# A hand-ordered attention and feed-forward kernel: the order of pairs 0 to 17 written anew, the first block of output weights requested right behind the input weights, and fewer products of zeros

## The chip, the cores and the metric

The kernel runs on one core of one Trainium2 chip. The metric is device time in microseconds. The kernel before takes 400.86 us, the median of three runs (400.78 to 400.98).

## The reference

Cosine attention for 8 batches and 12 heads, 448 positions, head size 64; then a feed-forward layer with a hard-swish over the 3584 rows of the attention's result.

```python
q_n = q / (norm(q, axis=-1) + 1e-6); k_n = k / (norm(k, axis=-1) + 1e-6)
attn = softmax(q_n @ k_n.T / 0.1)            # 448 x 448 for each head
x = (attn @ v) laid out as (8 * 448, 768)
h = x @ w_in                                 # 768 -> 2048
g = h * clip(h + 3, 0, 6) / 6
out = g @ w_out                              # 2048 -> 768
```

## The kernel before, in words

**Work.** Two heads of one batch make a pair; there are 48 pairs, six to a batch. The attention runs pair by pair, and the feed-forward layer of a batch runs in small units between later pairs. TensorE (PE) does all products and most transposes, ScalarE (ACT) the exponentials, VectorE (DVE) and GpSimd (POOL) most of the rest. SyncE (SP) issues the loads.

**The order is written out by hand.** Each engine executes its instructions in the order in which the program issues them, and the program issues them by tokens. Up to pair 17 the tokens stand in the text `PLAN`; from pair 18 (`FIRST`) on a loop produces them. A token is an operation and its arguments, and the letters v, p and a name the engine: DVE, POOL, ACT.

- `LQ.j` (L199) loads the queries or keys of item j in one 448 KB transfer; two items, 2d and 2d+1, serve the pairs 2d and 2d+1. `LV.d` (L214) loads the values of two pairs in four transfers. There are seven raw buffers: `LQ.j` waits until an earlier item's `NM` has read its buffer.
- `SQ.j.e.c.n` (L225 on ACT, L227 on POOL) squares n of seven columns from column c on; `RE.j` (L242, DVE) sums the squares; `BN`, `BS` (L248 to L254) do both by moments for three columns of item 1. `NO.d` (L278 to L285) takes the inverse norms of two items: a logarithm and an exponential on ACT, then two small operations on DVE (with v) or on ACT. `NM.j.e` (L295) multiplies an item by them. `VC.i` (L312, L314) casts the values of a pair.
- `TR.j` (L341, seven PE transposes into a PSUM bank), then `CQ.i`, `CK.i`, `CS.i` (L361, L363) copy the transposed queries and keys of pair i out of the bank. From item 14 on `XD.j` (L352) transposes by DMA instead.
- `SC.i.g` (L441, L444) are the four groups of score products of pair i, `EX.i.g` (L462, ACT) their exponentials, `VA.i.g` (L484) the products with the values into the bank pair `PV`, `FI.i` (L504, L505, DVE) the division by the sums. `BK.i` (L518, PE) and `CX.i` (L361, L363) turn the result into xT, the input of the feed-forward layer; `XP`, `XB` (L542, L530) do it by DMA.
- `UH.f.k` and `U` (L594) are the products of the feed-forward layer's first half, six to a block f of 128 columns; `UA` and `UV` do the ACT half (L611, "relu") and the DVE half (L617, "product") of the oldest open unit.
- `W` (L924, issued from POOL) requests one of twelve blocks of weights: eight of w_in, two for each quarter of its columns, then four of w_out.
- `D.n`, `DP.n`, `DQ.n` (L931, L937) are products of zeros, n of each; their result is read by nobody. DP and DQ write columns of PV that the sums leave free. A DQ works on 32-bit zeros and shows as two matmul rows in the trace.

**PSUM.** Of the eight banks two are PV. For the first six pairs four banks are the two score buffers SC0 and SC1 (two banks each, `SC.i.g.0` and `SC.i.g.1`), and Y and Z serve the transposes. At `OPEN` the SC banks become the banks M0 to M3, and all six (M0, M1, Y, Z, M2, M3; here numbered 0 to 5) go round as a ring: `SC` takes two (one for g = 3), and `TR`, `BK` and each unit one. A bank can be written again when its readers are done: for scores the exponentials on ACT, for a unit its relu on ACT and then its product on DVE.

Of the kernel before, what the change touches and what calls it, by code (L numbers as in the profile page):

```python
# [64 lines left out]
def kernel(
# [125 lines left out]
    def load_qk(j, *heads):  # L191
# [6 lines left out]
        g = slice(heads[0], heads[0] + 1) if heads else slice(0, 2)  # L198
        nc.sync.dma_start(out=raw_of[j][:, g, :, :].rearrange("p g c d -> p g (c d)"), in_=f[:, g, :])  # L199
        whole("LQ", j, heads or (0, 1))  # L200
        issued.update(("LQ", j, x) for x in heads or (0, 1))
# [916 lines left out]
```

## Time and profile before

| | |
|---|---|
| median of three runs | 400.86 us |
| the profiled execution's own time | 401.17 us |
| its span in the trace | 399.2 us |
| outside the span | 1.97 us |
| busy: PE, DVE, ACT, POOL | 98%, 74%, 69%, 59% |
| granted TensorE clock | full in all 40 slices of the page |
| matmul rows of products of zeros (L937, L931) | 65 and 1, of 3658 |

The page sums busy time over the whole span, but the kernel has a start in which queries and keys are prepared, a middle in which pairs and units alternate, and an end without attention. So the reading below is by stretches of time, each with the busy time of every engine. A busy time can hold overlaps: an instruction's start can lie before the end of the one ahead of it on the same engine, so the distance between starts is the better price of one more instruction. The chain of waits gives such distances for PE.

### The profile page before, as it was taken

How to read it: one execution, taken by the hardware profiler on the slowest of the kernel's cores; microseconds unless marked ns; L12 is line 12 of the kernel's file. 1: busy time of each engine (PE TensorE's matmuls, PEld its weight loads, DVE VectorE, ACT ScalarE, POOL GpSimd, SP SyncE). 2: the span in 40 equal slices, each digit the busy share in tenths (PEclk: the TensorE clock that was granted, in tenths of full speed). 3: DMA queues.
4: the chain of work that ended last, by engine and by line, in shares of the span. 5: the costliest groups of instructions: out<-in, count | busy, mean ns of one | idle time of the engine just before them, and what ended most of it. 6: DMA issues, size and time to landing. Idle time of an engine off the chain costs nothing.

```text
span 399.2 us, 9590 instructions
## 1 busy us (share of the span) xinstructions
PE 390.2 (98%) x3658; PEld 231.6 (58%) x3658; DVE 293.9 (74%) x537; ACT 276.9 (69%) x600; POOL 234.6 (59%) x234
## 2 busy tenths in 40 slices
PE   7999999999999999999999999999999999999996
PEld 5566556555565556555565556565565556555563
DVE  7998898999777787667767886686756566645663
ACT  5999889895768677777868769668648755235230
POOL 6999628662656988389368757767666400400070
PEclk9999999999999999999999999999999999999999
DMA  8999979988978868785887566795953423230133
GB/s 289 310 221 240 212 226 248 199 189 208 197 172 187 120 174 162 174 213 123 195 202 213 136 152 155 165 218 119 190 150 69 102 48 68 47 74 20 30 71 97
DMA packets 93165, 63.73 MB, mean 160 GB/s; under 512 B 56128, under 2 KB 93120, under 8 KB 93120
## 3 DMA queue, kind: packets, MB, share of 16 engines
q1 hardware_dynamic: 87408, 56.45, 60.4%
q0 software_dynamic: 5312, 6.29, 9.4%
q8 instruction: 28, 0.46, 0.5%
q10 hardware_dynamic: 400, 0.39, 0.3%
q14 instruction: 17, 0.14, 0.1%
HBM read 45.61 MB, written 11.01 MB: 142 GB/s over the span
## 4 chain that ended last, share of the span: by engine, by line
PE 92%; ACT 3%; DVE 2%; DMA 1%; issue 0%; POOL 0%; SPq 0%; DVEq 0%; ACTq 0%
PE M L594 25%; PE M L754 17%; PE PV L484 11%; PE Z L594 6%; PE Y L754 6%; PE M L444 5%; PE Y L594 5%; PE Z L754 5%; PE M L834 3%; ACT at L462 2%; DMA big<-in_k_dram 1%; PE Y L444 1%; PE Z L444 1%; PE Z L834 1%; PE PV L937 1%; PE SC L444 1%
## 5 line engine op out<-in xcount | busy, mean ns | idle before, releaser
L594 PE MATMUL M<-xT,w_in_sb 128*128 128x448 bf16 x540 | 114.6, 353 | 0.0
L462 ACT ACTIVATE at<-M 128x448 bf16<-128x448 f32 x195 | 96.6, 564 | 20.0 <-PE M L444 10.2
L594 PEld LDWEIGHTS <-w_in_sb 128*128 128x128 bf16 x768 | 72.2, 98 | 64.1 <-issue 3.8
L227 POOL TENSOR_TENSOR big<-big 128x896 f32<-128x896 f32 (+5 forms) x47 | 69.5, 1483 | 21.7 <-DMA big<-in_k_dram 12.0
L295 POOL TENSOR_TENSOR nrm<-big,r 128x896 bf16<-128x896 f32 (+1 forms) x45 | 75.7, 1683 | 6.5 <-ACT r L285 4.3
L617 DVE SCALAR_TENSOR_TENSOR gT<-u,M 128x448 bf16<-128x448 bf16 x80 | 49.0, 619 | 34.9 <-ACT u L611 34.3
L611 ACT ACTIVATE u<-M,bias 128x448 bf16<-128x448 f32 x90 | 58.0, 651 | 22.3 <-PE M L594 20.9
L484 PEld LDWEIGHTS <-at 128*128 128x128 bf16 (+1 forms) x1536 | 53.8, 97 | 20.5 <-issue 10.6
L484 PE MATMUL PV<-vx,at 128*128 128x65 bf16 (+1 forms) x1536 | 62.2, 193 | 0.0
L242 DVE TENSOR_REDUCE n<-big 128x14 f32<-128x896 f32 (+1 forms) x48 | 51.1, 1068 | 1.5 <-POOL big L227 1.5
L783 POOL TENSOR_TENSOR big<-big 128x384 f32<-128x384 f32 x12 | 13.0, 1080 | 58.9 <-ACT big L802 58.8
L401 POOL COPY km<-tT 64x128 bf16<-64x128 bf16 x34 | 12.8, 376 | 59.0 <-DMA tT<-nrm 24.9
L754 PEld LDWEIGHTS <-gT 128*128 128x128 bf16 x320 | 30.9, 98 | 21.4
L505 DVE TENSOR_TENSOR on<-PV,rc 128x512 bf16<-128x512 f32 x48 | 33.2, 692 | 1.7
L754 PEld LDWEIGHTS <-gs 128*128 128x128 bf16 x248 | 23.9, 98 | 16.0 <-issue 0.2
L462 ACT ACTIVATE at<-Y 128x448 bf16<-128x448 f32 x51 | 28.7, 564 | 6.1 <-PE Z L444 6.0
L754 PE MATMUL M<-w_out_sb,gT 128*128 128x384 bf16 x176 | 32.2, 326 | 0.0
L444 PE MATMUL M<-tT,kz 64*128 64x448 bf16 (+1 forms) x175 | 31.6, 351 | 0.3 <-ACT at L462 0.3
L462 ACT ACTIVATE at<-Z 128x448 bf16<-128x448 f32 x48 | 26.9, 561 | 4.2 <-PE M L444 2.1
L754 PE MATMUL M<-w_sum,gs 128*128 128x384 bf16 (+1 forms) x168 | 29.1, 318 | 0.0
L594 PE MATMUL Z<-xT,w_in_sb 128*128 128x448 bf16 x132 | 28.6, 352 | 0.0
L729 DVE TENSOR_TENSOR gs<-gT 128x1024 bf16<-128x1024 bf16 x30 | 26.3, 876 | 0.0
(135 smaller groups left out, 562.3 us busy)
## 6 DMA issues: line engine op xcount, KB each, us to landing
big<-in_k_dram SPq DMA_DIRECT2D x24, 448.0 KB, 4.4
big<-in_q_dram SPq DMA_DIRECT2D x24, 448.0 KB, 4.4
out_dram<-o SPq DMA_DIRECT2D x107, 96.0 KB, 2.2
big<-in_v_dram SPq DMA_DIRECT2D x48, 128.0 KB, 4.1
big<-in_v_dram SPq DMA_DIRECT2D x48, 96.0 KB, 4.1
w_in_sb<-in_moe_w_in_dram POOLq DMA_DIRECT2D x8, 384.0 KB, 8.3
w_out_sb<-in_moe_w_out_dram POOLq DMA_DIRECT2D x4, 768.0 KB, 11.0
tT<-nrm SPq DMA_TRANSPOSE x34, 3.2
```

What stands on the lines that cost most here:

```text
L227: engines[e].tensor_tensor(out=o, in0=i, in1=i, op=ALU.mult)
L242: nc.vector.tensor_reduce(out=sums_of(j, c0, n), in_=sq[:, :, c0 : c0 + n, :], axis=AX.X, op=ALU.add)
L295: engines[e].tensor_tensor(out=nrm[:, :, g, :].rearrange("p c g d -> p g c d"), in0=raw_of[j][:, g, :, :], in1=n2_and_r[2][:, d % 2, j % 2, :]
L444: nc.tensor.matmul(o, ks, qt[rows], start=True, stop=True)
L462: nc.scalar.activation(out=o, in_=x, func=AF.Exp, scale=inv_tau)
L484: nc.tensor.matmul(pv_out(j, h), at[rows, n, q_cols(i // HP, j)], vt[rows, 3 + h if name == "M" else 5 * h + int(name[1]), :], start=(name ...
L505: nc.vector.tensor_tensor(out=on[:, :, :, :].rearrange("p j h d -> p h j d"), in0=pv4[:, :, :, 0:D], in1=rc[:, :, :].to_broadcast([128, 2, ...
L594: nc.tensor.matmul(ps[:, 0:S], w_in_sb[:, cc, fc * 128 : (fc + 1) * 128], xT[b % 2][:, cc, 0:S], start=(cc == 0), stop=(cc == CC - 1), ski ...
L611: nc.scalar.activation(out=u[:, :], in_=ps[:, 0:S], func=AF.Relu, bias=half_bias, scale=1.0 / 6.0)
L617: nc.vector.scalar_tensor_tensor(out=g[:, fc, c0 : c0 + S], in0=u[:, :], scalar=1.0, in1=ps[:, 0:S], op0=ALU.min, op1=ALU.mult,)
L729: nc.vector.tensor_tensor(out=o[:, :, :], in0=x, in1=y, op=op)
L754: nc.tensor.matmul(m, lhs[:, c, :], rhs[:, c, c0 : c0 + width], start=(base is None and c == 0), stop=(c == KC - 1), skip_group_check=True,)
```

## The change

1. The tokens of pairs 0 to 17 stand in another order, and some work changes its engine. On ACT there are more squares (item 1's columns 3 and 4, the first half of items 5 and 7, all of item 13, but no longer those of items 8 and 15's first half), the casts of pairs 4, 8 and 9, and other copies. POOL gets the normalisation of items 11, 12 and of half of item 4, DVE gets the copies of pair 0.
2. `NO` is split into `NA` (the two ACT operations) and `NV` (the rest), so that other work can stand between them.
3. The ring of banks is no longer strictly in turn at the start: the text `RING` names a bank for each of the first allocations; after its end the ring goes round as before.
4. Products of zeros: D.1, 47 in DP and nine in DQ before; four in DP and fifteen in DQ (eleven of them first) now. The last one stands ahead of `SC.0.3`.
5. `LV.0` is issued ahead of `LQ.4`; `LQ.14`, `LV.5`, `LQ.16` and `LQ.15` ahead of `XP.6`.
6. On POOL's queue the first `W` of w_out stands behind the eighth of w_in with three operations between them, and the second nine operations further on; before, four operations stood between, and the second followed the first at once.

The rest of the edits makes the code able to do other things that this plan doesn't use (parts of a load, inverse norms in PSUM). From pair 18 on the program is unchanged.

```diff
 PLAN = [
-    "LQ.1 BN.1.0.3 DQ.9 SQ.1.p.3.2 SQ.1.a.5.2 BS.1.0.3 LQ.0 RE.1.3.4 SQ.0.p.0.3 LQ.3 SQ.3.p.0.4 SQ.0.a.3.4 RE.0 LQ.2",
-    "NO.0.1 NM.1.v.0 NM.1.v.1 SQ.3.a.4.3 NO.0.0 NM.0.p.1 SQ.2.a.4.3 TR.1.Z NM.0.p.0 LQ.5 SQ.2.a.0.4 D.1 DP.1 RE.3",
-    "CK.0.a SQ.5.p.0.4 SQ.5.a.4.3 RE.2 NO.1.v TR.0.Y LQ.4 CQ.0.a SQ.4.p.4.3 DP.2 SQ.4.a.0.4 DP.3 NM.3.p DP.1 RE.5",
-    "CQ.1.v RE.4 LV.0 SC.0.0.0 LQ.6 DP.3 VC.0.v NM.2.v.1 EX.0.0 SC.0.1.1 NM.2.p.0 CK.1.v LQ.7 LQ.8 DP.5 EX.0.1",
-    "SC.0.2.0 EX.0.2 DP.1 VC.1.v DP.1 DP.1 SC.0.3.1 EX.0.3 DP.2 VA.0.0 DP.2 LV.1 SQ.6.p.0.7 VA.0.1 SC.1.0.0 NO.2.v",
-    "NM.4.v.1 SC.1.1.1 TR.2.Y DP.1 NM.4.p.0 SQ.7.a.4.3 DP.1 RE.6 DP.1 DP.1 EX.1.0 EX.1.1 SC.1.2.0 TR.3.Z EX.1.2",
...
-    "NO.5.v BK.1.Y EX.4.3 SC.5.1.1 EX.5.0 SC.5.2.0 W TR.7.Z CX.1.v LQ.15 CK.6.v EX.5.1 VC.6.p VC.7.p EX.5.2 SC.5.3.1",
-    "CK.7.v VA.4.0 EX.5.3 VA.4.1 OPEN CS.7.v SC.6.0 EX.6.0 VA.4.2 VA.4.3.t CS.6.v FI.4 SC.6.1 EX.6.1 SC.6.2 SC.6.3",
-    "EX.6.2 TR.8 CQ.8.v BK.3 VA.5.0 CX.3.v W SQ.12.p.0.7 CQ.9.v VA.5.1 VA.5.2 VC.8.p EX.6.3 DP.1 BK.4.Y CX.4.v SC.7.0",
...
+    "LQ.1 SQ.1.a.5.2 LQ.0 BN.1.0.3 SQ.1.a.3.2 RE.1.3.4 BS.1.0.3 SQ.0.p.0.3 SQ.0.a.3.4 NA.0.1 NV.0.1 RE.0 LQ.3",
+    "SQ.3.p.0.4 NM.1.v.1 LQ.2 SQ.3.a.4.3 NM.1.v.0 NA.0.0 NV.0.0 LQ.5 RE.3 SQ.2.a.0.4 SQ.2.a.4.3 RE.2 NM.0.p.0",
+    "SQ.5.a.0.4 SQ.5.a.4.3 NM.0.p.1 DQ.11 TR.1 CK.0.v NA.1 DQ.2 TR.0 CQ.0.v DP.2 SC.0.0.0 NV.1.v LV.0 VC.0.p LQ.4",
+    "SQ.4.p.4.3 CQ.1.v SC.0.1.1 CK.1.a LQ.6 SQ.4.a.0.4 NM.3.p EX.0.0 DQ.2 SC.0.2.0 EX.0.1 DP.2 SC.0.3.1 RE.4 EX.0.2",
+    "RE.5 NM.2.v.1 NM.2.p.0 VA.0.0 LQ.8 SC.1.0.0 SQ.6.p.0.7 NA.2 NV.2.v EX.0.3 TR.3 LV.2 CK.2.v EX.1.0 SC.1.1.1 LQ.7",
+    "EX.1.1 TR.2 NM.4.p.1 VA.0.1 SC.1.2.0 NM.4.p.0 VA.0.2 EX.1.2 LV.1 W SQ.7.a.0.4 LQ.9 SQ.7.a.4.3 VA.0.3 VC.1.v",
...
+    "SC.4.3.1 EX.4.3 NM.7.p CX.2.v VC.4.a SC.5.0.0 TR.6 LV.4 EX.5.0 SC.5.1.1 RE.11 VA.4.0 CQ.6.v SC.5.2.0 EX.5.1",
+    "CQ.7.v BK.1 NV.4.v TR.7 EX.5.2 SC.5.3.1 VA.4.1 VA.4.2 LQ.13 EX.5.3 CX.1.v CK.6.v CK.7.v CS.6.v OPEN VA.4.3.t",
+    "SC.6.0 NM.8.p CS.7.v NM.9.p SC.6.1 VC.6.p SC.6.2 NA.5 EX.6.0 TR.8 SC.6.3 FI.4 CQ.9.v VA.5.0 EX.6.1 W W W CQ.8.v",
+    "BK.4 LQ.12 VA.5.1 CX.4.v BK.3 VA.5.2 CX.3.v VA.5.3.t SC.7.0 FI.5 VC.7.p EX.6.2 TR.9 EX.6.3 EX.7.0 SC.7.1 SC.7.2",
+    "EX.7.1 VA.6.0 CK.8.v EX.7.2 SC.7.3 EX.7.3 VA.6.1 LQ.14 SQ.12.p.0.7 W UH.0.0 CS.8.v BK.5 VA.6.2 CK.9.v CS.9.v",
+    "VA.6.3.t SC.8.0 CX.5.v UH.0.1 FI.6 UH.0.2 SC.8.1 EX.8.0 SC.8.2 NV.5.v EX.8.1 U UH.1.0 UH.2.0 UH.2.1 W NM.11.p.1",
+    "UH.1.1 UH.1.2 U UA SC.8.3 EX.8.2 UA UH.2.2 U NM.11.p.0 VA.7.0 UV UV VA.7.1 EX.8.3 VA.7.2 VA.7.3.t RE.12 SC.9.0",
+    "SQ.13.a.0.7 SC.9.1 EX.9.0 EX.9.1 SQ.14.p.0.7 FI.7 UH.3.0 UA UH.3.1 UH.3.2 U UA UV UV VC.8.a RE.13 U U VC.9.a UA",
+    "UA U W VA.8.0 NA.6 VA.8.1 NM.10.p VA.8.2 UV TR.10 LV.5 UV CQ.11.v SC.9.2 EX.9.2 VC.11.p VA.8.3.t SC.9.3 TR.11",
+    "NV.6.v U FI.8 VA.9.0 LQ.16 VA.9.1 UA VA.9.2 LQ.15 EX.9.3 VA.9.3.t CQ.10.v CK.10.a SQ.15.p.4.3 XP.6 NM.13.p UA",
+    "CK.11.v SC.10.0 U CS.10.v EX.10.0 RE.14.6.1 UV SC.10.1 UA CS.11.v UV VC.10.p FI.9 RE.14.0.6 SC.10.2 SQ.16.p.6.1",
...
 ]
+RING = "233232332323450123450350123451234502345012340123450125014012350123450..."
...
+        return ring[int(RING[n]) if n < len(RING) else (n - len(RING) + int(RING[-1]) + 1) % len(ring)]
...
     def norms(d, *items):
+        norms_root(d, *items)
+        norms_inverse(d, *items)
...
-    def busy(n):
-        bank_of("Y", 0)
-        for _ in range(n):
-            nc.tensor.matmul(Y[:, :], zeros[:, 0:128], zeros[:, :], start=True, stop=True)
```

More of the change, by code (lines that the diff above doesn't have):

```diff
@@ L21 @@
 PLAN = [
[39 rows of a table removed]
-]
[38 rows of a table added]
+]
+PLANNED = " ".join(PLAN).split()
+RING = "233232332323450123450350123451234502345012340123450125014012350123450123450135023451234015234501234501234501234501234501234501234501234501234501"
 @with_exitstack
@@ L157 @@
     Z = psum.tile([128, 512], FP32, name="Z", tag="Z")
-    ring = []
+    ring = [None, None, Y, Z, None, None]
     ring_n = [0]
     def next_bank():
+        n = ring_n[0]
         ring_n[0] += 1
-        return ring[(ring_n[0] - 1) % len(ring)]
+        return ring[int(RING[n]) if n < len(RING) else (n - len(RING) + int(RING[-1]) + 1) % len(ring)]
     raw_of, sq_of, nrm_of, at_of, on_of = {}, {}, {}, {}, {}
-    engines = {"v": nc.vector, "p": nc.gpsimd, "a": nc.scalar, "s": nc.sync}
+    engines = {"v": nc.vector, "w": nc.vector, "p": nc.gpsimd, "a": nc.scalar, "s": nc.sync}
     issued = set()
@@ L186, with load_qk @@
     MAIN = [0, 4, 1, 5, 2, 6]
-    def load_qk(j, *heads):
+    def load_qk(j, *part):
         needs(("NM", raw_before(j)))
@@ L197, in load_qk @@
         f = f.rearrange("n p g x -> (n p) g x")
[L198 to L201, printed above, removed]
+        c0, w = part or (0, 7)
+        o = raw_of[j][:, :, c0 : c0 + w, :].rearrange("p g c d -> p g (c d)")
+        nc.sync.dma_start(out=o, in_=f[:, :, c0 * D : (c0 + w) * D])
+        issued.update(("LQ", j, c) for c in range(c0, c0 + w))
     def load_v(d):
@@ L216, in square @@
     def square(j, e, c0, n):
-        needs(("RE", j - 2), ("LQ", j, 0), ("LQ", j, 1))
+        needs(("RE", j - 2), *(("LQ", j, c) for c in range(c0, c0 + n)))
         if j not in sq_of:
@@ L244, in moments @@
     def moments(j, c0, n):
-        needs(("RE", j - 2), ("LQ", j, 0), ("LQ", j, 1))
+        needs(("RE", j - 2), *(("LQ", j, c) for c in range(c0, c0 + n)))
         for c in range(c0, c0 + n):
@@ L254, in sums_of_moments, with norm_tiles, inverses, in_psum @@
         nc.vector.scalar_tensor_tensor(out=sums_of(j, c0, n), in0=mean, scalar=1.0, in1=m2, op0=ALU.mult, op1=ALU.add)
+    def norm_tiles(d, items):
+        items = tuple(x for x in items if x != "v") or (0, 1)
+        it = slice(items[0], items[-1] + 1)
+        return items, [t[:, d % 2, it, :] for t in n2_and_r], nr_eps[:, d % 2, it, :, :]
     def norms(d, *items):
-        on_vector, items = "v" in items, tuple(x for x in items if x != "v")
+        norms_root(d, *items)
+        norms_inverse(d, *items)
+    def inverses(j, g):
+        n = j // 2 % 2 * 2 + j % 2
+        c = slice(7 * g, 7 * g + 7)
+        if any(x in PLANNED for x in (f"NM.{j}.w", f"NM.{j}.w.{g}")):
+            return PV[:, 1, 264 + 14 * n : 278 + 14 * n][:, c]
+        return n2_and_r[2][:, j // 2 % 2, j % 2, c]
+    def in_psum(j):
+        return [any(x in PLANNED for x in (f"NM.{j}.w", f"NM.{j}.w.{g}")) for g in range(2)]
+    def norms_root(d, *items):
         needs(("NM", 2 * d - 4), ("NM", 2 * d - 3))
-        items = items or (0, 1)
+        items, tiles, pairs = norm_tiles(d, items)
         for x in items:
             needs(("RE", 2 * d + x))
-        it = slice(items[0], items[-1] + 1)
-        inverse([t[:, d % 2, it, :] for t in n2_and_r], nr_eps[:, d % 2, it, :, :], on_vector)
+        root(tiles, pairs)
+    def norms_inverse(d, *args):
+        items, tiles, pairs = norm_tiles(d, args)
+        le, r = tiles[1:]
+        parts = [(le, r)]
+        if any(any(in_psum(2 * d + x)) for x in items):
+            parts = []
+            for n, x in enumerate(items):
+                h = in_psum(2 * d + x)
+                n7 = PV[:, 1, 264 + 14 * (d % 2 * 2 + x) : 278 + 14 * (d % 2 * 2 + x)]
+                if h[0] == h[1]:
+                    parts.append((le[:, n, :], n7 if h[0] else r[:, n, :]))
+                else:
+                    for g in (0, 1) if h[0] else (1, 0):
+                        c = slice(7 * g, 7 * g + 7)
+                        parts.append((le[:, n, c], n7[:, c] if h[g] else r[:, n, c]))
+        inverse(tiles, pairs, "v" in args, parts)
         for x in items:
@@ L270, in norms_two, with root @@
         needs(*(("NM", 2 * d + x) for x in range(-4, 0)), *(("RE", 2 * d + x) for x in range(4)))
+        assert not any(any(in_psum(2 * d + x)) for x in range(4))
         two = [t.rearrange("p e i c -> p (e i) c") for t in n2_and_r]
-        inverse(two, nr_eps.rearrange("p e i c x -> p (e i) c x"), on_vector)
+        pairs = nr_eps.rearrange("p e i c x -> p (e i) c x")
+        root(two, pairs)
+        inverse(two, pairs, on_vector)
         issued.update(("NO", x, y) for x in (d, d + 1) for y in range(2))
-    def inverse(tiles, pairs, on_vector):
+    def root(tiles, pairs):
         n2, le, r = tiles
@@ L279, in inverse @@
         nc.scalar.activation(out=nr, in_=ln, func=AF.Exp, scale=0.5)
+    def inverse(tiles, pairs, on_vector, parts=None):
+        n2, le, r = tiles
+        nr = pairs[:, :, :, 0]
+        parts = parts or [(le, r)]
         if on_vector:
             nc.vector.tensor_reduce(out=le, in_=pairs, axis=AX.X, op=ALU.add)
-            nc.vector.reciprocal(out=r, in_=le)
         else:
             nc.scalar.activation(out=le, in_=nr, func=AF.Ln, bias=eps_bias)
-            nc.scalar.activation(out=r, in_=le, func=AF.Exp, scale=-1.0)
+        for x, o in parts:
+            if on_vector:
+                nc.vector.reciprocal(out=o, in_=x)
+            else:
+                nc.scalar.activation(out=o, in_=x, func=AF.Exp, scale=-1.0)
     def normalise(j, e, *heads):
@@ L294, in normalise @@
         n = len(heads)
+        assert e == "w" or not any(in_psum(j)[x] for x in heads)
+        if n == 1 or e == "w":
+            r = inverses(j, heads[0]) if n == 1 else PV[:, 1, 264 + 14 * (j % 4) : 278 + 14 * (j % 4)]
+        else:
+            r = n2_and_r[2][:, d % 2, j % 2, :]
         engines[e].tensor_tensor(
@@ L319, in bank_of @@
     def bank_of(name, reads):
-        bank = {"Y": Y, "Z": Z}[name] if name else next_bank()
+        bank = next_bank()
         key = id(bank)
@@ L948, in open_ring @@
         m = [psum_m.tile([128, 512], FP32, name=f"M{n}", tag=f"M{n}") for n in range(4)]
-        ring.extend([m[0], m[1], Y, Z, m[2], m[3]])
+        ring[:] = [m[0], m[1], Y, Z, m[2], m[3]]
     def unit():
@@ L974, in do @@
         key = (op,) + tuple(a for a in args if isinstance(a, int))
-        if op not in ("RE", "BN", "BS", "NM", "LQ"):
+        if op not in ("RE", "BN", "BS", "NM", "LQ", "NA", "NV"):
             issued.add(key[:3] if op == "SC" else key)
```

8 lines of the change are left out of this document (3 added, 5 removed), and 51 rows, old and new, of the table PLAN.

## The prediction

> **What bounds the kernel now.** I read the page's head first, then busy time by stretches of time, then what the products of zeros take of one stretch.
>
> ```profile
> span 399.2 us, 9590 instructions
> PE 390.2 (98%) x3658; PEld 231.6 (58%) x3658; DVE 293.9 (74%) x537; ACT 276.9 (69%) x600; POOL 234.6 (59%) x234
> PEclk9999999999999999999999999999999999999999
> ```
>
> ```profile
> 12.30:34.50 22.20, 21.02 (x285) 13.51 (x286) 21.62 (x50) 21.80 (x38) 22.16 (x19) 1.00 1.02 268
> 34.50:41.20 6.70, 6.58 (x125) 4.77 (x125) 5.39 (x20) 6.21 (x15) 6.69 (x9) 1.00 1.13 207
> 75.00:112.30 37.30, 37.17 (x346) 20.97 (x344) 32.14 (x55) 27.52 (x61) 17.37 (x18) 1.00 0.93 203
> ```
>
> ```profile
> 12.30:34.50 22.20, 6.66 (x39) 3.03 (x39) 1.00 1.02 268
> ```
>
> ```profile
> 17.25 0.42 PE PV L937 x4
> 35.48 0.19 PE Y L444
> 36.15 0.39 PE M L341 x7
> 39.53 0.96 PE PV L484 x32
> 57.43 1.14 PE M L594 x6
> ```
>
> The stretches' columns are length, then busy time of PE, weight loads, DVE, ACT and POOL, the granted clock, the DMA share and GB/s. PE looks full everywhere, but from 12.3 to 34.5 us, the first six pairs, 39 of its matmuls are products of zeros. Overlapped they count 6.66 us; the fourth fence, rows of the chain of waits (start, time, what), gives their real distance, 0.42/4 = 0.105 us, so 39 take 4.1 us. Useful PE time there is about 21.02 - 4.1 = 16.9 of 22.2 us. ACT, DVE and POOL are at 21.8, 21.6 and 22.2 of 22.2: **these three bound the first six pairs**, and the zeros lie in PE's holes. From 34.5 us on PE is full with useful work (6.58 of 6.70, 37.17 of 37.30), and there PE bounds. So taking zeros out is worth nothing by itself: it pays only as far as the first six pairs end sooner, or PE has more done when they end.
>
> **The change part by part.**
>
> *The first product, 0.* The wait that ends the start:
>
> ```profile
> 9.40 0.56 PE L341 MATMUL Z<-ident,nrm 128*128 128x128 bf16 x7 [1.53 <-DVE nrm L295]
> L937 PE MATMUL PV<-xT x12: 621/621/782, 1.2 to 5.9; 128*128 128x248 f32 x12
> L937 PE MATMUL PV<-xT x5: 372/373/373, 6.7 to 7.5; 128*128 128x248 f32 x5
> ```
>
> The first transpose waits at 9.40 us for DVE's normalised keys, and that chain (load, squares, norm, two halves on DVE) has the same links after the change. The first zeros grow from nine to eleven, 22 rows: the first thirteen at (5.9 - 1.2)/11 = 0.43, the rest at (7.5 - 6.7)/4 = 0.20 us end near 8.5, still under the cover of that wait. If the cover were gone the four more rows would cost 0.8 us. The later zeros are pairs of products: two DQ take 4 x 0.20 = 0.8 each and stand ahead of `TR.0`, which waits for POOL, and of `SC.0.2`, which waits for an exponential of 0.9; the four DP take 0.4 in such holes. Splitting `NO` leaves the same four instructions, so it costs nothing by itself; where it puts them is in the sums below.
>
> *`LQ.4` behind `LV.0`, +0.9 at the first exponential.*
>
> ```profile
> 3.29 0.48 SPq L199 DMA_DIRECT2D big<-in_q_dram  x1
> 3.81 2.92 SPq L214 DMA_DIRECT2D big<-in_v_dram  x4
> 12.17 0.63 ACT L225 ACTIVATE big<-big 128x512 f32<-128x512 f32 x1
> 12.72 3.01 ACT L462 ACTIVATE at<-SC 128x896 bf16<-128x896 f32 x4
> 10.00:15.00 5.00, 4.17 (x34) 2.21 (x33) 4.41 (x8) 4.56 (x9) 5.00 (x6) 1.00 1.07 325
> ```
>
> `LQ.4` went out at 3.29 and its square started on ACT at 12.17 without a wait; the exponentials follow at 12.72. Now 448 KB of values go ahead of it, 0.459 MB/325 GB/s = 1.4 us with the DMA engines full (1.07). The bounds are 0 (it may have landed long before 12.17) and +1.4; I take +0.9, nearer the full row. The same square's other part stands on POOL, ahead of `NM.3`, so POOL moves with it. The added ACT work ahead of it (a 0.42 and a 0.63 us square) fits in waits for loads.
>
> *ACT from the first to the last exponential of pair 5, -0.8.*
>
> ```profile
> L462 ACT ACTIVATE at<-SC 128x896 bf16<-128x896 f32 x18 | 15.5, 918 | 0.1
> L278 ACT ACTIVATE n<-n 128x28 f32<-128x28 f32 x4 | 0.9, 234 | 0.0
> L279 ACT ACTIVATE nr<-n 128x28 f32<-128x28 f32 x4 | 0.9, 230 | 0.1
> L361 ACT COPY xT<-Z 128x448 bf16<-128x448 bf16 x1 | 0.5, 513 | 0.0
> ```
>
> ```profile
> L314 ACT CAST vx<-big 128x512 bf16<-128x512 f32 x3 | 1.9, 642 | 0.0
> ```
>
> The same 24 exponentials and four squares of equal size stand there. `NA.5` leaves (0.234 + 0.230), `CX.0` leaves (0.513), the cast of pair 4 comes (0.642): -0.33. Before, ACT was idle for 22.2 - 21.8 = 0.4 us; if the new order closes all of it, -0.4 more. So ACT would end pair 5 at +0.1.
>
> *POOL to item 7, +0.5.* In the new order POOL does, from `SQ.4` to `NM.7`, four whole and three half normalisations, three whole squares, three smaller ones, three weight requests and a cast:
>
> ```profile
> L295 POOL TENSOR_TENSOR nrm<-big,r 128x896 bf16<-128x896 f32 x6 | 10.1, 1689 | 0.0
> L227 POOL TENSOR_TENSOR big<-big 128x896 f32<-128x896 f32 x3 | 5.4, 1805 | 0.0
> L924 POOL DMA_DIRECT2D w_in_sb<-in_moe_w_in_dram x4 | 3.0, 738 | 0.0
> L295 POOL TENSOR_TENSOR nrm<-big,r 128x448 bf16<-128x448 f32 x2 | 2.3, 1130 | 0.0
> L314 POOL CAST vx<-big 128x512 bf16<-128x512 f32 x3 | 1.8, 615 | 0.0
> L227 POOL TENSOR_TENSOR big<-big 128x384 f32<-128x384 f32 x2 | 1.7, 832 | 0.0
> L227 POOL TENSOR_TENSOR big<-big 128x512 f32<-128x512 f32 x1 | 1.0, 1036 | 0.0
> ```
>
> ```profile
> 28.42 1.68 POOL L295 TENSOR_TENSOR nrm<-big,r 128x896 bf16<-128x896 f32 x1
> 32.81 0.55 PE L341 MATMUL Z<-ident,nrm 128*128 128x128 bf16 x7
> 34.53 0.37 PE L444 MATMUL M<-tT,kz 64*128 64x448 bf16 x2 [0.27 <-ACT at L462]
> ```
>
> 4 x 1.69 + 3 x 1.13 + 3 x 1.81 + 1.04 + 2 x 0.83 + 3 x 0.74 + 0.62 = 21.1, less about 0.6 for 17 starts some 0.04 ahead of the previous end: 20.5. From 13.1 it ends at 33.6. Before, `NM.7` ended at 28.42 + 1.68 = 30.1 and its transposes started at 32.81, so it had 2.7 us to spare; now item 7's transposes cannot start before 33.6, 0.8 later, and pair 5's last scores stand behind them on PE. Before, pair 6 started at 34.53, 1.7 after those transposes; now only the last scores and one exponential (about 0.5 + 0.55) lie between. That gives 34.7 to 35.1, against 34.6 by ACT. I take **+0.4** for pair 6's start, with -0.6 (`LQ.4` no later) and +1.0 (+1.4 for `LQ.4`) as bounds.
>
> *What PE has done by then, -0.6.* `VA.4.2` and `VA.4.3`, sixteen matmuls, now stand ahead of pair 6's first scores, 16 x 0.96/32 = 0.48, and one product of zeros behind it is gone, 0.105.
>
> *Pairs 6 to 8, +0.3.* The named banks are reused sooner. `SC.6.2` takes the bank of `TR.7`, whose four copies on DVE come late with it, `SC.7.2` one of `SC.7.0`, `SC.8.0` one of `SC.7.2`. In each case PE waits for ACT or DVE to read the bank. I estimate 0.1 each, up to one 0.55 us exponential each.
>
> *Units and later pairs, -0.1.*
>
> ```profile
> 41.20:56.00 14.80, 14.73 (x176) 8.62 (x173) 12.93 (x27) 12.73 (x28) 5.46 (x6) 1.00 0.97 175
> 56.00:75.00 19.00, 18.95 (x198) 10.80 (x197) 17.29 (x36) 17.50 (x38) 16.08 (x15) 1.00 1.14 248
> ```
>
> PE's useful work is the same, and before it had 0.07 + 0.05 us of holes; nothing is left to gain. The moved squares and casts load ACT more, which PE's saturation hides (price below, among the rivals). The earlier w_out request adds 768 KB of traffic nobody waits for: its sums come past 75 us. And SP:
>
> ```profile
> SPq L542 <- DVE on L505: 12.0, 1, 12.0
> ```
>
> SP's queue stood 12.0 us behind `XP.6`, with `LQ.14` and `LQ.16` behind it; they now go ahead. PE hardly had holes from this, so no gain is counted.
>
> **Sum**: 0 + 0.4 - 0.6 + 0.3 - 0.1 = 0.0. The profiled execution, 401.17 us (span 399.2 and 1.97 around it), stays 401.2; it lies 0.31 above the median of 400.86, so the forecast is **400.9**.
>
> **The rivals.**
>
> *ACT becomes the bound behind the banks (slower).* From 41.2 to 75 ACT has 12.73 + 17.50 = 30.2 of 33.8 us. The moves add a whole square (0.63 for 512 elements, so some 1.0), two casts (1.28) and about two copies (1.0), less a 0.63 square: 2.7, or 97%. `SC.10.1` now takes both banks of `SC.10.0` with one unit (six matmuls, 1.14 us) between, and the unit of block 7 takes one of `SC.9.2` with `VA`, `SC.9.3` and `TR.11` between, 0.24 + 0.19 + 0.39. An exponential pair takes 1.0. From the point where ACT lags by more than 0.2 us, every such place costs about 0.5; four of them and three weight requests bunched behind `NM.9` make +1.5: 402.4. For it: 97%. Against it: ACT's hand-summed order still meets each bank. Weights late for the unit of block 4 would give about the same.
>
> *The start isn't late (faster).* If `LQ.4` lands before ACT and POOL get to it, both are 0.9 earlier and POOL's chain holds nobody: -0.9 and -0.3 of the bank waits: 399.7. For it: DMA's total is unchanged. Against it: the DMA share of 1.07.
>
> *The clock falls (slower).* PE's holes are left empty. Cold products took 0.43 against 0.20 us in the rows above, so twice. Useful PE time is 16.9/22.2 = 0.76 of the stretch, 1.52 at half clock; over the 5.4 us from 1.2 to 6.6 for which the first products ran cold, 0.52 x 5.4 = +2.8: 403.7. Against it: the 1.53 us hole at 9.40 left the clock full. The Trainium skill, "TensorE: Matmul & The Clock Gate", section Why this matters for your kernels, asks for no PE-idle gaps over about 3 us between bursts. By that rule nothing falls here, since my longest hole is some 1.5 us; the trace agrees as far as it goes.
>
> **How the numbers follow.** The measurement can tell about 0.2%, 0.8 us. Forecast 0.40, ACT and banks 0.32, clock 0.03, early start 0.25. The range runs from the faster rival to just above the slower one's 402.4: 399.6 to 402.8. Faster 0.25, same 0.40, slower 0.35; the forecast's own range is 400.1 to 401.7.
>
> **What would show it.** `SQ.4` on ACT waiting for a DMA until about 13; item 7's transposes near 33.6; pair 6's first scores at 34.9; clock full in every slice; pair 18's first scores near 112.3 as now. I am wrong if pair 6 starts outside 34.2 to 35.5, or if PE shows over 0.5 us of waits for ACT between 41 and 112.

## The result and the profile after

The changed kernel takes 403.41 us (median of six runs, 402.76 to 404.54) where the kernel before takes 400.92: a ratio of 1.0061, 95% interval 1.0043 to 1.0079. It is slower by 0.6%, some 2.5 us, outside the range given. The profiled execution took 404.25 us, its span 402.3.

The page's head, and the clock's digits from its second part:

```profile
span 402.3 us, 9532 instructions
PE 389.7 (97%) x3626; PEld 230.5 (57%) x3626; DVE 290.5 (72%) x531; ACT 278.7 (69%) x605; POOL 237.5 (59%) x236
PEclk9899999999999999999999999999999999999999
```

PE has 32 matmul rows fewer, the zeros, and is busy 0.5 us less; the span is 3.1 us longer. The second digit of the clock is an 8, where before had nines only. The rows on which the prediction hung, from the timelines of PE and ACT (start, time, what, and in brackets the idle time ahead and what ended it):

```profile
8.97 0.56 PE L392 MATMUL Y<-ident,nrm 128*128 128x128 bf16 x7 [1.50 <-DVE nrm L348]
12.29 0.63 ACT L228 ACTIVATE big<-big 128x512 f32<-128x512 f32 x1 [0.25 <-DMA big<-in_q_dram]
32.91 0.55 PE L392 MATMUL Y<-ident,nrm 128*128 128x128 bf16 x7
34.43 0.35 PE L495 MATMUL Z<-tT,kz 64*128 64x448 bf16 x1
115.32 0.36 PE L495 MATMUL Y<-tT,kz 64*128 64x448 bf16 x1
```

And pair 18's first scores before:

```profile
112.28 0.55 PE L444 MATMUL M<-tT,kz 64*128 64x448 bf16 x4
```

Item 1 is transposed at 8.97 (9.40 before), `SQ.4` on ACT waits for its load only until 12.29, item 7 is transposed at 32.91 and pair 6 starts at 34.43, 0.1 sooner than before, with all of pair 4's sums done. So the start is not what is lost. But pair 18's first scores, with which the unchanged part of the program begins, come at 115.32 instead of 112.28: **all of the loss, +3.04 us, lies between 34.4 and 115.3.** From pair 6 to pair 18 the changed kernel takes 80.89 us, where before took 77.75. The waits of PE from 34 to 112 us (waited for, total, times, longest), first of before, then of after:

```profile
PE M L444 <- ACT at L462: 0.3, 1, 0.3
```

```profile
PE M L495 <- DVE gT L668: 1.6, 2, 1.1
PE M L645 <- DMA w_in_sb<-in_moe_w_in_dram: 0.5, 1, 0.5
PE M L645 <- DVE gT L668: 0.4, 2, 0.2
```

Five waits, 2.5 us. A wait costs more than its idle time, since matmuls that follow closely overlap (the six of a unit start 0.19 apart and last 0.35, so 0.16 goes as well): 2.5 + 5 x 0.16 = 3.3 us. The one wait of before, 0.27, stands right ahead of its pair 6 at 34.53; behind it there is none. So the waits are large enough for the whole loss. Where each comes from, by PE's timeline:

```profile
48.05 1.30 PE L645 MATMUL M<-xT,w_in_sb 128*128 128x448 bf16 x6 [0.53 <-DMA w_in_sb<-in_moe_w_in_dram]
58.04 2.43 PE L645 MATMUL M<-xT,w_in_sb 128*128 128x448 bf16 x12 [0.19 <-DVE gT L668]
72.74 0.37 PE L495 MATMUL M<-tT,kz 64*128 64x448 bf16 x2 [1.12 <-DVE gT L668]
88.12 0.35 PE L495 MATMUL M<-tT,kz 64*128 64x448 bf16 x1 [0.51 <-DVE gT L668]
88.65 1.29 PE L645 MATMUL M<-xT,w_in_sb 128*128 128x448 bf16 x6 [0.19 <-DVE gT L668]
```

**The wait at 48.05** is the unit of block 4, for the fourth block of w_in. The chain of waits has that request at 37.00 and 10.91 us to its landing; the eight requests took 11.4 us in the median, 8.3 before. **The wait at 58.04**, 0.19, stays in nearly every version below and is left aside.

**The wait at 72.74** is `SC.13.0`, whose bank was a unit's. The chain of waits up to it:

```profile
68.04 1.49 POOL big L230
69.53 0.02 issue
69.55 2.08 DVE n L245 x2
71.63 1.07 DVE gT L668 x2
72.70 0.04 issue
72.74 0.37 PE M L495 x2
```

The unit's product stands on DVE behind two sums of squares (`RE.16`, `RE.17`), and these waited for POOL's `SQ.16`. On POOL, `SQ.17` and a weight request stand ahead of it:

```profile
65.59 1.68 POOL L230 TENSOR_TENSOR big<-big 128x896 f32<-128x896 f32 x1 [6.09 <-DVE gT L668]
67.21 0.81 POOL L975 DMA_DIRECT2D w_out_sb<-in_moe_w_out_dram  x1
68.04 1.48 POOL L230 TENSOR_TENSOR big<-big 128x768 f32<-128x768 f32 x1
```

POOL sat idle for 6.09 us. (That alone costs nothing: before, it stood idle for 8.52 us up to 57.32, and PE had no wait behind it.) The name in the bracket is an inference; what `SQ.17` needs is `LQ.17`, and SP's queue with the landing of that request gives the true one:

```profile
47.60 1.37 SPq L593 DMA_TRANSPOSE xT<-on  x1
50.98 0.38 SPq L203 DMA_DIRECT2D big<-in_q_dram  x1
51.41 0.45 SPq L203 DMA_DIRECT2D big<-in_k_dram  x1
51.91 4.03 SPq L217 DMA_DIRECT2D big<-in_v_dram  x4
58.53 0.77 SPq L203 DMA_DIRECT2D big<-in_q_dram  x1
big<-in_q_dram SPq DMA_DIRECT2D x1, 448.0 KB, 14.5
```

`LQ.17` (50.98) took 14.5 us, so it landed at 65.5. `LQ.18` took 15.9, `LQ.19` 11.3. The transposing DMA ahead of them, `XP.6`, went out at 47.60 and took 12.9 us; before, it went out at 51.68 and took 3.1. The two landings, after and before:

```profile
xT<-on SPq DMA_TRANSPOSE x1, 12.9
```

```profile
xT<-on SPq DMA_TRANSPOSE x1, 3.1
```

In these microseconds the DMA engines were busy and moved little; the rows by stretches end with the DMA share and GB/s, first after, then before:

```profile
52.00:56.00 4.00, 4.00 (x77) 2.90 (x73) 2.47 (x9) 2.84 (x6) 2.46 (x3) 1.00 1.07 64
56.00:60.00 4.00, 3.81 (x23) 1.83 (x22) 3.86 (x10) 3.58 (x8) 3.10 (x4) 1.00 1.56 97
```

```profile
52.00:56.00 4.00, 3.93 (x76) 2.60 (x72) 3.91 (x10) 3.04 (x7) 0.00 (x0) 1.00 0.70 140
56.00:60.00 4.00, 4.00 (x24) 1.85 (x23) 3.88 (x8) 3.74 (x9) 2.68 (x2) 1.00 1.05 393
```

A full share at 64 and 97 GB/s is not a lack of work: the transfers stand in each other's way, which I call the collision. Two requests are new there: the first of w_out, at 48.40 on POOL (60.59 before), which took 17.5 us, and `XP.6` itself, 4.1 us sooner (51.68 before), while the last of w_in are still on their way.

**The waits at 88.12 and 88.65** are for products behind late relus. ACT, its queue in order, stood still ahead of them:

```profile
85.39 0.62 ACT L365 CAST vx<-big 128x512 bf16<-128x512 f32 x1 [1.76 <-DMA big<-in_v_dram]
```

`VC.15` waited for `LV.7`. On SP's queue its four parts went out from 75.09 on:

```profile
75.09 2.59 SPq L217 DMA_DIRECT2D big<-in_v_dram  x4
```

The last left at 77.08. They went beside two requests of w_out and took up to 7.9 us. Before, they had gone out from 60.4 to 65.4. In the new order `LV.7` stands behind `NM.18`, and so behind `XD.14` and `XD.15` on SP's queue. Neither my account of the change nor my prediction names this move.

### The profile page after: what moved, and what is told of

It reads as the page before. It is cut to its first block, busy times and chain, and to the rows that moved or that the text cites. A ratio compares the mean times of both kernels' runs of the same rounds, so it can differ in the third digit from the quotient of the medians.

```text
span 402.3 us, 9532 instructions
## 1 busy us (share of the span) xinstructions
PE 389.7 (97%) x3626; PEld 230.5 (57%) x3626; DVE 290.5 (72%) x531; ACT 278.7 (69%) x605; POOL 237.5 (59%) x236
## 4 chain that ended last, share of the span: by engine, by line
PE 80%; DVE 6%; DMA 6%; ACT 3%; issue 2%; POOL 2%; SPq 0%; POOLq 0%; ACTq 0%; DVEq 0%
PE M L645 19%; PE M L805 19%; PE PV L535 9%; PE Y L645 6%; PE Z L645 6%; PE Z L805 5%; PE M L885 5%; PE M L495 4%; PE Y L805 4%; DMA w_in_sb<-in_moe_w_in_dram 3%; DMA big<-in_v_dram 2%; DVE n L245 2%; ACT at L513 2%; DVE gT L668 1%; PE Y L495 1%
## 5 line engine op out<-in xcount | busy, mean ns | idle before, releaser
L645 PE MATMUL M<-xT,w_in_sb 128*128 128x448 bf16 x504 | 107.3, 352 | 0.9 <-DMA w_in_sb<-in_moe_w_in_dram 0.5
L348 POOL TENSOR_TENSOR nrm<-big,r 128x896 bf16<-128x896 f32 (+1 forms) x49 | 79.3, 1625 | 10.6 <-ACT r L333 6.1
L230 POOL TENSOR_TENSOR big<-big 128x896 f32<-128x896 f32 (+4 forms) x45 | 67.3, 1497 | 17.9 <-DVE gT L668 6.1
L662 ACT ACTIVATE u<-M,bias 128x448 bf16<-128x448 f32 x84 | 54.5, 657 | 23.6 <-PE M L645 23.1
L668 DVE SCALAR_TENSOR_TENSOR gT<-u,M 128x448 bf16<-128x448 bf16 x73 | 44.3, 618 | 30.3 <-ACT u L662 29.7
L245 DVE TENSOR_REDUCE n<-big 128x14 f32<-128x896 f32 (+3 forms) x49 | 51.4, 1052 | 4.0 <-POOL big L230 3.7
L452 POOL COPY km<-tT 64x128 bf16<-64x128 bf16 x34 | 13.1, 387 | 57.9 <-PE M L495 29.4
L805 PE MATMUL M<-w_out_sb,gT 128*128 128x384 bf16 x224 | 40.5, 326 | 0.0
L805 PEld LDWEIGHTS <-gs 128*128 128x128 bf16 x248 | 23.8, 98 | 16.3 <-DVE gs L780 0.4
L513 ACT ACTIVATE at<-Z 128x448 bf16<-128x448 f32 x51 | 28.8, 565 | 1.7 <-PE M L495 1.7
L645 PE MATMUL Z<-xT,w_in_sb 128*128 128x448 bf16 x138 | 29.9, 352 | 0.0
L645 PE MATMUL Y<-xT,w_in_sb 128*128 128x448 bf16 x126 | 27.3, 352 | 0.0
## 6 DMA issues: line engine op xcount, KB each, us to landing
w_in_sb<-in_moe_w_in_dram POOLq DMA_DIRECT2D x8, 384.0 KB, 11.4
```

The lines of the kernel that those rows point to most:

```text
L230: engines[e].tensor_tensor(out=o, in0=i, in1=i, op=ALU.mult)
L245: nc.vector.tensor_reduce(out=sums_of(j, c0, n), in_=sq[:, :, c0 : c0 + n, :], axis=AX.X, op=ALU.add)
L348: engines[e].tensor_tensor(out=nrm[:, :, g, :].rearrange("p c g d -> p g c d"), in0=raw_of[j][:, g, :, :], in1=r.rearrange("p (g c) -> p g ...
L513: nc.scalar.activation(out=o, in_=x, func=AF.Exp, scale=inv_tau)
L645: nc.tensor.matmul(ps[:, 0:S], w_in_sb[:, cc, fc * 128 : (fc + 1) * 128], xT[b % 2][:, cc, 0:S], start=(cc == 0), stop=(cc == CC - 1), ski ...
L662: nc.scalar.activation(out=u[:, :], in_=ps[:, 0:S], func=AF.Relu, bias=half_bias, scale=1.0 / 6.0)
```

## The experiments

The theory: **late transfers**, three of them, make the loss: `XP.6` and the first w_out request meet, `LV.7` is asked for late, the fourth w_in block is bunched. The rivals: **ACT is the bound** (the prediction's), and **the clock** falls. The before kernel ran beside each; there its own runs went from 400.6 to 405.6, so ratios have intervals of about 0.3% to each side, and the trace (plan end: pair 18's first scores) is the second measure. A trace is of one execution; e1's is of its fastest (401.81, the median being 404.11). Of the plan's lines only the tokens round an edit are shown.

**Single moves.**

e1_wout_late:

```diff
-    "UA U W VA.8.0 NA.6
+    "UA U VA.8.0 NA.6
-    SC.11.2 TR.13 SQ.15.p.0.4 RE.15
+    SC.11.2 TR.13 SQ.15.p.0.4 W RE.15
```

> The changed kernel with the first output-weight request alone put 11 us later on POOL's queue (behind SQ.15.p.0.4, near 59.5 us, where POOL idles for 6.1 us). Theory 'collision': the request of 48.4 us and the transposition XP.6 of 47.6 us are in the 16 DMA engines together, the transposition takes 12.9 us where it took 3.1, and LQ.17, LQ.18, LV.6 and LQ.19 behind it take 11 to 16 us. With the request gone, XP.6 lands in 3 to 6 us, LQ.17 in under 9, POOL's idle time before SQ.17 is gone, and SC.13.0's wait of 1.1 us with it: 1.0 to 1.5 us faster than the changed kernel, near 402.1. The wait of 0.5 at unit 4 stays, and so may the 1.8 us that ACT waits for LV.7. Rival 'the transposition is too early whatever the output weights do' (the last input weights are in flight until 53): XP.6 still takes over 8 us, and the time moves by less than 0.4. Rival 'ACT bound': the loads get shorter and the wait at SC.13.0 stays, since ACT is as full; within 0.4 of 403.4.

e3_xp6_late:

```diff
-    CK.10.a SQ.15.p.4.3 XP.6 NM.13.p UA
+    CK.10.a SQ.15.p.4.3 NM.13.p UA
-    LQ.18 VA.10.3.t
+    LQ.18 XP.6 VA.10.3.t
```

> The changed kernel with the transposition XP.6 alone put behind LQ.17 and LQ.18 on SP's queue (from 47.6 to some 52 us), the first output-weight request staying at 48.4. Theory 'collision' in its plain form: LQ.17 and LQ.18 no longer stand behind the transposition, and land in 6 to 9 us; XP.6 itself still meets the output weights and takes over 6 us, which nothing waits for until 73 us. SQ.17 starts by 60, SC.13.0's wait goes: 1.0 to 1.4 us faster, near 402.2. Rival 'output weights alone fill the engines': without XP.6 ahead the loads still take over 11 us, and the time stays within 0.4 of 403.4.

Measured: e1 1.0044 [1.0018, 1.0070], e3 1.0011 [0.9985, 1.0038]. What is left of PE's waits from 34 to 112 us, e1 and then e3:

```profile
PE M L645 <- DVE gT L668: 0.4, 2, 0.2
PE M L645 <- DMA w_in_sb<-in_moe_w_in_dram: 0.3, 1, 0.3
PE M L495 <- DVE gT L668: 0.3, 1, 0.3
```

```profile
PE M L645 <- DMA w_in_sb<-in_moe_w_in_dram: 0.6, 1, 0.6
PE M L645 <- DVE gT L668: 0.4, 2, 0.2
```

`SC.13.0`'s wait is gone in both, with either partner moved; `LQ.17` took 8.0 and 7.3 us. Plan ends at 112.99 and 113.02, some 2.3 sooner than in the changed kernel, of which the start gives 0.5 (pair 6 at 33.9 in both). But `XP.6` still took 9.2 and 10.8 us, not the 3 to 6 I expected of e1: it is slow beside w_in's end (e1) as beside w_out's first block (e3), and that by itself delays nobody. The time of e1 can't be told from the changed kernel's, so for e1 trace and time disagree, and why is open; the time of e3 lies 2.0 us below it by the two ratios, the forecast being 1.0 to 1.4.

e2_v7_early:

```diff
-    SQ.17.p.0.7 LV.6",
+    SQ.17.p.0.7 LV.6 LV.7",
-    NM.18.p UV UV LV.7 VC.14.p
+    NM.18.p UV UV VC.14.p
```

> The changed kernel with the value load LV.7 alone put right behind LV.6 on SP's queue (near 56 us, was 75.1). Theory 'late load': ACT's conversion VC.15.a stands at 83.6 us and waits 1.8 us for LV.7, which was asked for beside two output weights; the relus behind it keep the banks of SC.14.2 and SC.14.3 for 0.7 us and more. With the load early this wait goes: 0.7 to 1.1 us faster than the changed kernel, near 402.4. Rival 'ACT bound': ACT has other work to do up to there, and the banks come free only 0.3 us sooner: 403.1. The wait of 1.1 us at SC.13.0 stays by both.

Measured: 1.0221 [1.0177, 1.0265], a miss of both. SP's queue in its trace:

```profile
55.45 16.30 SPq L217 DMA_DIRECT2D big<-in_v_dram  x8
71.85 0.54 SPq L203 DMA_DIRECT2D big<-in_q_dram  x1
```

Eight requests took SP 16.3 us to put out, where four took 4.03, and `LQ.19` went out at 71.85 instead of 58.53. The last three parts of `LV.7` left at 63.60, 68.75 and 71.16, just as `XP.6` (63.6), `LQ.17` (68.7) and `LQ.18` (71.1) landed. Each time eight requests were out, and the next one went when the oldest was back. So more requests into jammed engines hold up those behind them. Whether the limit of eight is the queue's or the program's, no run shows.

e4_act_back (six tokens):

```diff
-    SQ.13.a.0.7   VC.8.a   VC.9.a   CQ.13.a   CK.13.a   CX.8.a
+    SQ.13.p.0.7   VC.8.p   VC.9.p   CQ.13.v   CK.13.v   CX.8.v
```

> The changed kernel with the work that went to ACT given back: SQ.13, VC.8 and VC.9 to POOL, CX.8, CK.13 and CQ.13 to DVE, 3.4 us of ACT's work between 41 and 75 us. Rival 'ACT becomes the bound behind the banks' of the prediction: SC.13.0's wait of 1.1 us and the losses round it go, 1.0 to 1.5 us faster, near 402.2. Theory 'late loads': SC.13.0 waits for products that stand on DVE behind RE.16 and RE.17, and these for POOL's squares, which stand behind a load that lands 14.5 us after its request; ACT's work doesn't enter, and the time stays within 0.4 of 403.4.

Measured: 1.0065 [1.0035, 1.0094], as the changed kernel. In its one trace `SC.13.0` waits less and plan end is 114.57, but the time doesn't follow: ACT's added work is not the 2.5 us.

**The changed kernel again, and the request in the kernel before.**

> The changed kernel once more, beside the runs below on the same chip. All theories: 2.0 to 2.8 us over the kernel before. If the granted clock falls near 11 us in its trace again, that is a property of the kernel; if it doesn't, of where the run's 3.41 us windows of the clock happen to lie, and pair 6 starts some 0.5 us sooner (33.9).

Measured: 1.0063 [1.0026, 1.0099]. `LQ.17` took 14.0 us, `SC.13.0` waited 1.3: the collision comes back. The clock fell at 11.1 us again, this time for 6.8 us, and pair 6 started at 36.11.

e5_before_wout_early, an edit of the kernel before:

```diff
-    SQ.15.p.4.3 FI.7
+    SQ.15.p.4.3 W FI.7
-    CK.10.a LQ.16 W UA
+    CK.10.a LQ.16 UA
```

> The kernel before with only its first output-weight request put at the end of the input weights (behind SQ.15.p.4.3, 47.2 us; was 60.6). Theory 'collision': the transposition XP.6 of 51.7 us now meets the output weights, takes over 6 us (was 3.1), the five loads behind it take over 9 us (were 4 to 8), and POOL, which already idles 8.5 us for them there, idles longer: 1 to 3 us slower than before, with waits of PE for the products' banks between 60 and 76. Rival 'nobody waits for that traffic', the prediction's step: within 0.3 of before.

Measured: 1.0033 [1.0007, 1.0060]. `XP.6` took 5.2 us, the loads behind it 5.2 to 9.1 (over 9 was expected), and no wait of PE between 60 and 76 came. The trace says that the early request alone costs nothing there, against my theory; the ratio says 0.1 to 0.6%. That stays open.

e9_wout_ahead, the changed kernel with the request still earlier:

```diff
-    UH.2.0 UH.2.1 W NM.11.p.1
+    UH.2.0 UH.2.1 W W NM.11.p.1
```

(and the `W` of e1's first line gone).

> The changed kernel with the first output-weight request put earlier still, right behind the last input weights (42.6 us, was 48.4), so five microseconds ahead of the transposition XP.6 instead of 0.8 behind it. Theory 'a request that POOL makes while the transposition is in the engines': as in the kernel before with the same request early, XP.6 lands in under 7 us and LQ.17 in under 9, SC.13.0 waits under 0.4; 1.0 to 1.5 us faster than the changed kernel, although the output weights are asked for sooner. Theory 'the traffic itself': XP.6 meets the input weights' end and all of the output weights; it takes over 9 us, LQ.17 over 11, and the time stays within 0.5 of the changed kernel's or is longer.

Measured: 1.0025 [0.9988, 1.0061]. `XP.6` took 12.6 us and `LQ.17` 11.2, as the theory of the traffic had it, but no wait at `SC.13.0`, as the other had it. Its start came late (pair 6 at 37.21): `LQ.17` landed at 64.1, 1.4 us sooner than in the changed kernel, in a plan that ran 2.8 later. Neither theory is borne out as it was put.

**Four moves.** Those of e1 and e3, and:

```diff
-    "SC.4.3.1 EX.4.3 NM.7.p CX.2.v
+    "SC.4.3.1 EX.4.3 NM.7.p W CX.2.v
-    VA.5.0 EX.6.1 W W W CQ.8.v
+    VA.5.0 EX.6.1 W W CQ.8.v
-    "VC.12.p LQ.19 UV XD.14
+    "VC.12.p LQ.19 LV.7 UV XD.14
-    NM.18.p UV UV LV.7 VC.14.p
+    NM.18.p UV UV VC.14.p
```

> The changed kernel with four requests moved and nothing else: the first output weights behind SQ.15.p.0.4, XP.6 behind LQ.18, the fourth input weights behind NM.7 (POOL idles 0.8 us there), LV.7 behind LQ.19. Theory 'late transfers': unit 4's wait, SC.13.0's and the 0.8 us at SC.14.2 and SC.14.3 all go, and the lead of 0.7 to 1.3 us at pair 6 is kept up to pair 18, whose first scores come at 111.0 to 111.8 (112.28 before): 0.4 to 1.2 us faster than before. Rival 'full engines' (ACT or DVE are the bound somewhere between 41 and 112 whatever the loads do): the lead is eaten, and it ends within 0.3 of before or slower.

> The four moves once more, beside the kernel with the zeros, on the same chip. Both theories: 0 to 1.5 us over before's median, with some runs near a span of 398.7 at the full clock and some near 402.5 at a mean clock of 0.987 to 0.996.

Measured: 1.0028 [0.9995, 1.0060] and 0.9984 [0.9957, 1.0012]. Between 34 and 112 us only the wait of 0.19 is left (58.04 in the changed kernel); plan ends at 111.66 and 111.59. From pair 6 to pair 18 e6 takes 77.71 us, 3.18 less than the changed kernel, and the four waits that are gone are 2.35 + 4 x 0.16 = 3.0 of that. The loss is gone, so it lay in four requests; the order of the work itself costs nothing. It gains nothing either: the 0.4 to 1.2 us that I forecast for e6 don't show.

**One of the four left out.**

> The four moves without that of the output weights: the first request stays at 48 us, XP.6 comes behind LQ.17 and LQ.18. Theory 'only the two together': the loads land in under 10 us, no wait at SC.13.0, plan end within 0.3 us of the four moves' (111.6 to 111.7 where the start is undisturbed), time within 0.5. Rival 'the early request costs by itself', by the traffic ahead of LQ.17 to LQ.19: LQ.17 over 11 us and a wait of 0.5 or more at SC.13.0, or 1 us and more in the time.

> The four moves without that of LV.7, which stays behind NM.18. Theory 'late load': SC.14.2 or SC.14.3 wait 0.6 to 0.9 us again behind ACT's VC.15.a, plan end 0.6 to 0.9 later than with the four moves, as much in the time. Rival 'with the other loads in time LV.7 is too, since XD.14 ahead of it on SP's queue comes sooner': within 0.3.

> The four moves without that of the fourth input weights, which are asked for at 37 us with two others. Theory 'bunched weights': unit 4 waits 0.3 to 0.6 us for them, and plan end is 0.3 to 0.6 later than with the four moves. Rival 'the slack further on takes it up': the wait is there, but plan end within 0.2 of the four moves'.

> The four moves without that of XP.6, which stays at 47 us ahead of LQ.17; the output weights come later. Theory 'only the two together': XP.6 takes 7 to 10 us against the end of the input weights, LQ.17 under 9, a wait of at most 0.3 at SC.13.0; plan end within 0.4 of the four moves'. Rival 'the transposition alone': a wait of 0.8 or more at SC.13.0.

Measured, with plan end: f1 1.0002 [0.9976, 1.0029], 111.74; f2 1.0048 [1.0013, 1.0082]; f3 1.0021 [0.9993, 1.0049]; f4 1.0000 [0.9977, 1.0022], 111.72. With `XP.6` out of the way the early request costs 0.08 us of plan end, and with the request later `XP.6`'s place costs 0.06: **in this order of work it takes both to make the wait.** They don't make it always: e9 had both, and no wait. Leaving `LV.7` late costs 0.1 to 0.8% in f2, whose executions spread from 401.2 to 410.6. Its price in time isn't settled, as e3, at 0.1%, leaves it late too, with one wait of 0.19 behind it in its trace. ACT in f2:

```profile
89.04 0.62 ACT L365 CAST vx<-big 128x512 bf16<-128x512 f32 x1 [4.36 <-DMA big<-in_v_dram]
```

The wait has the same place as in the changed kernel. Its length I don't use, since that execution (span 407.4) was longer than most of f2's. In f3 the wait for w_in didn't come: its request went out at 39.56, 2.6 us later than in the changed kernel, as pair 6 started later (36.98), but it took 8.8 us, not 10.9. Of the eleven traces that ask for this block as the changed kernel does, four show the wait, of 0.3 to 0.6 us.

**Two moves.** g1_two_moves has `XP.6`'s and `LV.7`'s, g2_v7_only the latter.

> The changed kernel with XP.6 behind LQ.18 and LV.7 behind LQ.19, and nothing else: output weights and fourth input weights asked for as in the changed kernel. Theory 'XP.6 meeting the output weights, and LV.7 late': at most a wait of 0.6 at unit 4 is left, plan end between 111.6 and 112.3 where the start is undisturbed, time within 0.3% of before. Rival 'the early output weights or the bunched input weights matter after all': a median 1 us and more above before's, with waits that show which.

> The changed kernel with LV.7 behind LQ.19 alone. Theory 'two separate losses': no wait at SC.14.2 and SC.14.3, the wait of 1 us and more at SC.13.0 stays, 0.7 to 1.5 us faster than the changed kernel, so 1.0 to 1.9 above before. Rival 'SP's queue fills again, as with LV.7 behind LV.6': LQ.21 late, over 5 us slower than before.

Measured: g1 0.9990 [0.9959, 1.0021], one wait of 0.2 left, and

```profile
111.80 0.36 PE L495 MATMUL Y<-tT,kz 64*128 64x448 bf16 x1
```

against 115.32. g2 1.0071 [1.0046, 1.0097]: the waits at `SC.14.2` are gone from the trace and the one at `SC.13.0` (1.3) stays, but the time didn't fall by the 0.7 us I forecast. Its four parts of `LV.7` took SP 8.65 us to put out, from 59.92 on, held up as in e2. PE waited 0.43 at 101.86 for a later transposing DMA, which went out at 95.55 and took 6.2 us (95.26 and 4.6 in the changed kernel); what made it slower isn't shown. With the collision there, neither of the two earlier places of `LV.7` that I tried gains; without it, two moves are enough in the time, and g1's trace shows no wait for w_in. No version beats the kernel before by more than its interval.

**The clock.** e7_more_zeros:

```diff
-    NM.0.p.1 DQ.11 TR.1 CK.0.v NA.1 DQ.2 TR.0
+    NM.0.p.1 DQ.13 TR.1 CK.0.v NA.1 DQ.3 TR.0
```

> The changed kernel with three more products of zeros where PE idles: 13 instead of 11 ahead of TR.1, 3 instead of 2 behind it. Theory 'share of the window': the clock halves after a window of 3.41 us in which PE was busy for under half (0.43 in the changed kernel's 7.5 to 10.9 us), and these fill that window to over 0.7; no fall near 11 us, pair 6 at 33.9, and the median 0.2 to 0.6 us below the changed kernel's. Rival: the clock's fall costs nothing, as ACT and the loads set the start; within 0.2 of the changed kernel. The late waits (unit 4, SC.13.0, SC.14.3) stay by both.

Measured: 1.0110 [1.0078, 1.0143]. As expected the clock stayed full at 11 us and pair 6 started at 33.96; but the jam was no shorter (`LQ.17` took 15.0). `SC.13.0` waited 1.8, in a hole so wide that the clock fell there:

```profile
70.77:74.18 3.41, 1.57 (x30) 1.22 (x30) 3.38 (x7) 1.99 (x5) 3.41 (x4) 1.00 1.20 202
74.18:77.59 3.41, 3.41 (x32) 1.59 (x29) 2.71 (x5) 2.81 (x6) 3.11 (x4) 0.50 1.12 203
```

e8_moves_and_zeros has the four moves and these zeros; e10_before_zeros gives the kernel before `DQ.11` for its `DQ.9`, and `DP.6` for its first `DP.1`.

> The changed kernel with the four requests moved and the three products of zeros added. Theory 'two costs, late transfers and the granted clock': PE has no hole of the start that is under half busy in any 3.41 us (0.86 at least, as with the zeros alone) and none later (the transfers are in time), so the clock stays full in nearly every run; all runs lie near the 398.7 us span that the undisturbed runs of the four moves had, so 0.4 to 1.0 us under the median of before, and 1.5 to 2.5 us under the median of the four moves alone. Rival 'the clock falls elsewhere or costs nothing': as the four moves alone, within 0.5 us of that.

> The kernel before with more products of zeros in its first hole: 11 instead of 9 of the long kind ahead of TR.1, 6 instead of 1 of the short kind ahead of TR.0. Theory 'share of the window': its hole of 7.9 to 9.4 us, with under half of a window's 3.41 us busy in the worst place, no longer halves the clock in any run: median 0.3 to 1.0 us below before, its lowest runs as before's. Rival 'the clock's falls come from elsewhere, or cost nothing': the same median within 0.2.

Measured: e8 0.9991 [0.9962, 1.0020], e10 0.9994 [0.9965, 1.0022]. Neither gained what the theory gave: e8's median is that of the four moves beside it (401.09 both), e10's within 0.3 of before. What the clock's falls cost in the median is not shown.

## Why the prediction was wrong

- *The first product, 0*: right, 0.4 better. The zeros ended at 7.47, not near 8.5, as the clock was full from 4.08 on.
- *`LQ.4` behind `LV.0`*: mis-sized; the first exponential came at 13.03, 0.3 later than before (12.72) and not 0.9. The load landed at 12.29, near my lower bound.
- *ACT* and *POOL to item 7*, +0.4 together: pair 6 started at 34.43, so -0.1. POOL's chain was right in kind and mis-sized: it began at 12.41, not 13.1, took 20.0 us, not 20.5, and item 7's transposes came at 32.91, not 33.6. With the start unchanged and the clock full it began at 33.9 to 34.1 in seven traces, and at 37.2 in an eighth, whose first loads landed late.
- *What PE has done by then*, -0.6: right in kind, pair 4's sums stand ahead of pair 6. From pair 6 to pair 18 e6 takes 77.71 us with one wait of 0.19 + 0.16 and before 77.75 without, so some 0.4.
- *Pairs 6 to 8*, +0.3: no wait of PE is listed there; the size is not settled.
- ***Units and later pairs*, -0.1: this is the step that failed; the runs show +3.3 us of waits in its place, where before had none, and 3.0 of them go when four requests are moved.** It said that "the earlier w_out request adds 768 KB of traffic nobody waits for". Nobody waits for the weights, but what stands in the same engines beside them, `XP.6` and the loads behind it, is waited for at `SC.13.0`, four links on: load, POOL, DVE, bank. It noted that loads now go ahead of `XP.6` (`LQ.14` and `LQ.16`; the `LV.5` and `LQ.15` that the change lists stood ahead of it before as well) and counted that as harmless. It didn't ask what `XP.6`, sooner now, meets (w_in's end and, 0.8 us behind it, w_out's first block) and who is behind it (`LQ.17`, which POOL's order puts ahead of `SQ.16`). And it never looked at `LV.7`, whose place on SP's queue moved by 10 to 15 us: a token among many, with ACT's cast in order ahead of the relus.
- That ACT's added work is hidden held: giving it back gained nothing (e4). So the rival *ACT becomes the bound* had a wrong mechanism, though its side remark of late weights for the unit of block 4 came true with 0.53 us.
- *The clock falls*, 0.03: the longest hole of the start was 1.5 us, as it said, and the clock fell all the same, for one stretch of 3.41 us; pair 6 then began some 0.4 us later than in the traces without. That the measured time lies near this rival's 403.7 is chance, since the fall made pair 6 only some 0.4 of the 2.5 us later.
- Its tests of being wrong gave no sign (pair 6 inside 34.2 to 35.5, no wait for ACT listed between 41 and 112). They looked at the start and at one engine, and the loss came through the queues. Of what it said would show it, the clock and pair 18's first scores came out otherwise.

The forecast's sum priced instructions on engines; of transfers it priced `LQ.4` alone. The change moved a few requests past one another, and there it lost.
